# Gate and Up of the fourth token tile by Strassen's seven products, in a fused attention and gated feed-forward kernel

## The chip, the cores and the metric

The kernel runs on one core of a Trainium2 chip. Its time is the device time of one execution in microseconds, the median of several. TensorE (PE) multiplies matrices into banks of PSUM, VectorE (DVE) and ScalarE (ACT) read and empty those banks, GpSimd (POOL) works on SBUF alone, and SyncE (SP) issues the DMAs. Each engine takes its instructions in the order in which they stand in its queue; an instruction that has to wait holds up everything behind it on its engine.

## The reference

`x` has 2048 tokens of 512 elements. Both branches read the same normalised tokens. The inner width of the feed-forward, 1792, is 14 blocks of 128.

```python
xn = layernorm(x)                                  # 2048 x 512
q, k, v = split(xn @ wqkv)                         # 32 heads of 16
p = softmax(mask(q @ k.T * 16**-0.5))              # causal, window of 256
s = (p @ v) @ wo
gate, up = xn @ w1, xn @ w3                        # 2048 x 1792 each
h = silu(gate) * up
out = x + s * silu(h @ w2)
```

## The kernel before

Every float32 operand of a large product is split into two fp16 parts, high and low, and a product is made of three (high by high, low by high, high by low), so that one 128 by 128 block costs three matmuls.

The tokens are worked in four tiles of 512 (t = 0 to 3). The attention is cut into 32 units: a tile, a group of 8 heads and one half of it. A unit brings small score pieces (score products for the maxima, L671, and for the exponentials, L759) and one set of value products (L787), and around them stands dense work: projections (L601), values (L567), Gate and Up (L1059), Down (L1284, L1202) and the output projection (L1336). `spread` deals the dense pieces out between the score pieces of a unit, by a cost per piece; `feed_forward` lists the feed-forward's pieces, and each unit takes its share of the total. PE runs in exactly the order in which the program records its instructions. On the other engines a list scheduler sets the order, and pieces under `urgent()` go first.

`gate_up(t, f)` makes Gate, then Up, of one block f for all 512 tokens: 12 matmuls of 512 columns each, half of them per piece, into one PSUM bank. `bank()` hands out two banks in turn, m0 and m1, to all dense work. Gate is emptied by a tanh on ACT (L1074) and a product on DVE (L1078), Up by a product on DVE (L1083), which gives h.

Down is a plain product in tiles 0 and 1 (L1284). In tiles 2 and 3 it is already made by seven products: `fold_first` and `fold_second` form sums of h on POOL and split them into high and low parts (casts on ACT L1114 or POOL L1116, low parts on POOL L1117, sums L1125 and L1140 to L1142), `fold_weights` has made the sums of w2, and `fold_down_piece` runs the products (L1202, 256 columns each), which `unfold` adds up. Blocks 0 to 7 are one set of seven products, blocks 8 to 13 the second, in the order 0, 6, 3, 4, 5, 1, 2; the second set of tile 3 stands at the kernel's end, followed by the last output projections.

The scores of the exponentials go through a mask on DVE (L766) and an exponential on ACT (L769); the maxima are DVE instructions (L685). SBUF tiles named slot are one pool of 54, taken and given back.

## Time and profile before

| | |
|---|---|
| time, median of 3 runs | 803.87 us (803.73 to 803.97) |
| the profiled execution, first to last instruction (span) | 801.8 us |
| granted TensorE clock | 1.000 |
| PE busy | 791.1 us, 99% |
| DVE, ACT, POOL busy | 623.0, 393.9, 381.2 us (78, 49, 48%) |
| DMA | 134.18 MB, 167 GB/s in the mean |

The profile gives the profiled execution's own time as its span; the runs' median lies 2.07 us above that, which is what lies around the first and the last instruction. A row of a timeline gives the start, the length, the engine, the line and operation, what is written from what, and the count; in brackets stands how long the engine idled before it, and what ended that. Matmuls overlap: a 256-column matmul is listed with 0.27 us, but the next starts much earlier, so their cost is read from start to start.

### The profile page before, as it was taken

The page shows a single profiled execution, that of the slowest core. Times are in us where ns is not written, and L with a number is a line of the kernel's source. Part 1 is how long each engine was busy: PE and PEld are TensorE (multiplying, and loading weights), DVE is VectorE, ACT ScalarE, POOL GpSimd, SP SyncE. Part 2 cuts the span into 40 slices and gives each one's busy share as a digit, 9 for nine tenths or more (in the row PEclk, how much of TensorE's full clock was granted, in tenths as well). Part 3 has the DMA queues.
Part 4 walks back from the last instruction along what each step waited for, and adds up shares of the span by engine and source line. Part 5 has one row for each costly group of instructions (what it writes and reads, how often), then busy time and mean ns, then how long its engine had stood idle before and what let it go on. Part 6 is the DMA issues. An engine that isn't in the chain of part 4 may idle for free.

```text
span 801.8 us, 23974 instructions
## 1 busy us (share of the span) xinstructions
PE 791.1 (99%) x9181; PEld 403.8 (50%) x9181; DVE 623.0 (78%) x2005; ACT 393.9 (49%) x592; POOL 381.2 (48%) x746
## 2 busy tenths in 40 slices
PE   8999999999999999999999999999999999999997
PEld 4443445444454444444445444466544744466465
DVE  8887889778797778787888887776678876874537
ACT  6989777744355544344443344344434334444411
POOL 2355657633229435365442546330446276650770
PEclk9999999999999999999999999999999999999999
DMA  9987654636666565657555733665453553334431
GB/s 281 245 258 238 196 185 144 248 111 208 173 215 189 169 210 144 214 148 258 130 194 173 213 114 101 177 173 157 137 159 87 159 157 110 89 117 134 129 94 56
DMA packets 109858, 134.18 MB, mean 167 GB/s; under 512 B 18928, under 2 KB 64944, under 8 KB 109744
## 3 DMA queue, kind: packets, MB, share of 16 engines
q1 hardware_dynamic: 109456, 132.13, 55.4%
q8 instruction: 72, 1.18, 0.6%
q10 hardware_dynamic: 288, 0.52, 0.2%
q14 instruction: 42, 0.34, 0.1%
HBM read 91.23 MB, written 36.57 MB: 159 GB/s over the span
## 4 chain that ended last, share of the span: by engine, by line
PE 80%; DVE 8%; DMA 4%; ACT 3%; issue 2%; POOL 1%; SPq 1%; DVEq 0%; ACTq 0%; POOLq 0%
PE m L1059 31%; PE po L787 9%; PE m L601 8%; PE m L1202 8%; PE m L1284 7%; PE s L759 5%; PE m L1336 4%; PE m L567 4%; PE s L671 3%; DMA slot<-in_B_w_dram 2%; DVE junk L685 2%; PE po L671 2%; ACT sqa L249 1%; DVE s L766 1%; POOL slot L345 1%
## 5 line engine op out<-in xcount | busy, mean ns | idle before, releaser
L1059 PE MATMUL m<-XH,slot 128*128 128x512 f16 x896 | 267.3, 380 | 1.1 <-DVE slot L1078 0.6
L769 ACT ACTIVATE pt<-s,es 128x1024 f32<-128x1024 f32 x152 | 167.6, 1112 | 178.7 <-DVE s L766 176.9
L1059 PEld LDWEIGHTS <-slot 128*128 128x128 f16 x1344 | 124.9, 98 | 155.6 <-issue 13.1
L1059 PE MATMUL m<-XL,slot 128*128 128x512 f16 x448 | 169.8, 379 | 0.0
L766 DVE TENSOR_TENSOR s<-s,MK 128x256 f32<-128x256 f32 (+2 forms) x280 | 118.7, 434 | 53.5 <-PE s L759 49.8
L685 DVE CUSTOM_DVE_ANT_0 junk<-s,MW 128x320 bf16<-128x320 f32 x276 | 133.9, 485 | 18.4 <-PE s L671 11.4
L339 POOL TENSOR_TENSOR slot<-slot,slot 128x256 f16<-128x256 f32 (+1 forms) x86 | 57.6, 692 | 128.8 <-ACT slot L1092 60.0
L345 POOL TENSOR_TENSOR slot<-slot,slot 128x128 f16<-128x128 f32 x168 | 68.9, 444 | 76.6 <-ACT slot L343 76.6
L685 DVE CUSTOM_DVE_ANT_0 junk<-po,MW 128x320 bf16<-128x320 f32 x172 | 83.4, 485 | 4.6
L1284 PE MATMUL m<-slot,slot 128*128 128x512 f16 x336 | 78.5, 380 | 1.1 <-DVE slot L1078 1.1
L787 PE MATMUL po<-pt,V 64*32 64x320 f32 (+4 forms) x2880 | 77.2, 342 | 0.1
L601 PE MATMUL m<-XH,slot 128*128 128x512 f16 x240 | 70.8, 380 | 0.5 <-DVE slot L1078 0.5
L1202 PE MATMUL m<-slot,slot 128*128 128x256 f16 x588 | 68.4, 273 | 0.0
L1074 ACT ACTIVATE slot<-m,sgs 128x512 f32<-128x512 f32 x56 | 38.3, 684 | 59.8 <-PE m L1059 59.7
L1117 POOL TENSOR_TENSOR slot<-slot,slot 128x256 f16<-128x256 f32 x98 | 64.6, 671 | 1.1
L1202 PEld LDWEIGHTS <-slot 128*128 128x128 f16 x588 | 56.2, 98 | 11.5 <-issue 2.8
L787 PEld LDWEIGHTS po<-pt,V 64*32 64x32 f32 x2880 | 50.4, 106 | 22.4 <-issue 0.8
L1078 DVE SCALAR_TENSOR_TENSOR slot<-slot,m 128x512 f32<-128x512 f32 x56 | 38.3, 684 | 28.9 <-ACT slot L1074 26.7
L759 PE MATMUL s<-qa,KA 50*64 50x320 f16 (+3 forms) x1472 | 58.3, 259 | 0.0
L601 PEld LDWEIGHTS <-slot 128*128 128x128 f16 x392 | 36.5, 98 | 42.6 <-issue 1.7
L759 PEld LDWEIGHTS <-KA 50*64 50x64 f16 x1472 | 30.1, 105 | 51.7 <-issue 32.8
L1284 PEld LDWEIGHTS <-slot 128*128 128x128 f16 x336 | 30.7, 98 | 39.2 <-issue 4.7
(194 smaller groups left out, 1131.5 us busy)
## 6 DMA issues: line engine op xcount, KB each, us to landing
slot<-dW SPq DMA_DIRECT2D x98, 256.0 KB
slot<-in_B_w_dram SPq DMA_DIRECT2D x56, 256.0 KB
slot<-dFold SPq DMA_DIRECT2D x48, 256.0 KB
dW<-slot SPq DMA_DIRECT2D x42, 256.0 KB
slot<-in_A_x_dram SPq DMA_DIRECT2D x30, 256.0 KB
KA<-dK SPq DMA_DIRECT2D x24, 288.0 KB
slot<-dWQ SPq DMA_DIRECT2D x24, 256.0 KB
qa<-dQ SPq DMA_DIRECT2D x30, 192.0 KB
```

What stands on the lines that cost most here:

```text
L339: op(out[:, c], a[:, c], b[:, c])
L345: nc.gpsimd.tensor_sub(lo[:, c:c + P], raw[:, c:c + P], hi[:, c:c + P])
L601: nc.tensor.matmul(cell["pp"][:, cols[n]], w[:, (a * NC + c) * P:(a * NC + c + 1) * P], b[:, c, cols[n]], start=n == 0 and (c, i) == parts ...
L685: lasts["maximum"] = nc.vector.tensor_tensor_reduce(out=junk[:, :n], in0=s[:, r, :n], in1=mask, scale=1.0, scalar=NEG, op0=ALU.add, op1=AL ...
L759: nc.tensor.matmul(s[64 * h:64 * h + 64, r, o:o + 64 * n], ka[rows, 2 * p + a, 64 * (m + 4):64 * (m + 5)], qa[rows, 2 * p + a, 64 * (m + k ...
L766: nc.vector.tensor_add(v, v, MK[:, kind, of:of + n, :].unsqueeze(1).to_broadcast([P, 2 * len(which), n, 64]))
L769: lasts["exp"] = nc.scalar.activation(pt, s, AF.Exp, scale=es)
L787: nc.tensor.matmul(cell["po"][32 * i:32 * i + 32, h, 64 * (m + k):64 * (m + k + n)], V[64 * h:64 * h + 64, (4 * t + m // 2) % VB, hd * VW: ...
L1059: nc.tensor.matmul(cell[k], w[:, (a * NC + c) * P:(a * NC + c + 1) * P], b[:, c, :], start=c == 0 and i == 0, stop=c == NC - 1 and i == 2)
L1117: nc.gpsimd.tensor_sub(lo, view, hi)
L1202: nc.tensor.matmul(cell["ps"][:, c], made[:, f:f + P], wj[:, g:g + 256], start=j == j0 and c == 0 and n == 0, stop=j == j1 - 1 and n == 2, ...
L1284: nc.tensor.matmul(ps, hh[:, a * TW + b * P:a * TW + (b + 1) * P], w[:, c * D:(c + 1) * D], start=f == f0 and i == 0, stop=f == f1 - 1 and ...
```

## The change

Only the fourth tile's Gate and Up are changed. Two neighbouring blocks 2j and 2j+1 are taken together (a quad, j = 0 to 6). The weights of such a pair are a 2 by 2 arrangement (two halves of the 512 inputs by two blocks), the tokens another (two halves of the inputs by two halves of 256 tokens), and their product is made by seven products in place of eight, in Winograd's form with shared sums. One product is Gate in columns 0 to 255 and Up in columns 256 to 511 of one bank: 12 matmuls of 256 columns. Only products 1, 2 and 4 read plain weights; the sums of w1 and w3 are made on POOL in tiles 1 and 2 (`weight_sums`) and stored to DRAM, the sums of the tokens in tile 2 (`token_sums`).

The seven products stand in the order p1, p2, p6, p5, p7, p3, p4. p1, p6, p5 and p3 add up in one bank, m0, which the quad keeps (`retained`), and after each of them ACT copies the running sum out (L1421). p2, p7 and p4 go to the other bank; DVE adds one of those copies to them (L1426). Half a block of Gate and Up then lies in SBUF, and gets a tanh on ACT (L1436), a product on DVE (L1439) and one on POOL (L1440). `arranged` and `in_runs` place the quad's pieces among the other dense pieces: p1 with p2, p6 alone, p5 with p7, p3 with p4.

The scale of the normalised tokens is halved (XS) so that sums fit fp16, the weights' blocks are stored in another column order (`split_blocks`), the fold takes halves of the tokens in place of every second 128, and the third tile's output projections stand one unit later.

```diff
-XS = 2.0**10
+XS = 2.0**9
+QUAD_FROM = 3
+QUAD_AT = ((1, 10), (1, 13), (2, 1), (2, 3), (2, 5), (2, 7), (2, 9))
+HALVES_AT = {3: (2, 11)}
...
     def bank(shape, dtype=F32):
-        open_bank[0] = b = 1 - open_bank[0]
+        open_bank[0] = b = 1 - (open_bank[0] if retained[0] is None else retained[0])
...
+    def weight_sums(j):
...
+        def scale(i, k):
+            raw = cell["raw"][i][k]
+            with behind_exp():
+                nc.scalar.activation(raw, raw, AF.Copy, scale=inverses[:, j, k, i:i + 1])
+
+        def sums(k):
+            a, b = (cell["raw"][i][k] for i in range(2))
+            add(b[:, r], b[:, l], b[:, r])
+            sub(b[:, l], a[:, l], b[:, l])
+            sub(a[:, l], b[:, r], a[:, l])
+            sub(a[:, r], a[:, r], a[:, l])
+
+        def cut(i, k):
+            raw = cell["raw"][i][k]
+            made = take(F16)
+            with behind_exp():
+                nc.scalar.copy(made[:, 0:512], raw)
+            halves(sub, made[:, 512:], raw, made[:, 0:512])
...
+    LOADS = ((0,), (1,), (3, 4), (5, 6), (), (), (2,))
+
+    def quad(t, j):
...
+        def product(ps, w, x, first):
+            for k in range(2):
+                for c in range(2):
+                    for n, (a, b) in enumerate(((0, 0), (1, 0), (0, 1))):
+                        nc.tensor.matmul(ps[:, 256 * k:256 * k + 256], w(k, a, c), x(b, c),
+                                         start=first and k == 0 and c == 0 and n == 0,
+                                         stop=k == 1 and c == 1 and n == 2, skip_group_check=True)
+
+        def copied(ps):
+            made = take(F32)
+            with urgent():
+                lasts["exp"] = nc.scalar.activation(made, ps, AF.Copy, scale=CS)
+            return made
+
+        def added(ps, other):
+            with urgent():
+                lasts["emptied"] = nc.vector.scalar_tensor_tensor(other, ps, CS, other, op0=ALU.mult, op1=ALU.add)
+            return other
+
+        def activated(f, half, made, done_with=True):
...
+            nc.scalar.activation(h, made[:, 0:256], AF.Tanh, scale=sg_apart[:, f:f + 1])
+
+            def gated():
+                nc.vector.scalar_tensor_tensor(h, h, 1.0, made[:, 0:256], op0=ALU.add, op1=ALU.mult)
+                nc.gpsimd.tensor_mul(h, h, made[:, 256:512])
+                give(made, after=10)
+            later(1, gated)
...
+        def p6():
+            product(cell["a"], summed_up(0, 0), token_sum(1, 256), False)
+            cell["u2"] = copied(cell["a"])
+
+        def p5():
+            product(cell["a"], summed_up(1, 256), token_sum(0, 0), False)
+            cell["v5"] = copied(cell["a"])
+
+        def p7():
+            cell["b"] = bank([P, 512])
+            product(cell["b"], summed_up(1, 0), token_sum(0, 256), True)
+            give(QW[t, j, 5], QW[t, j, 6])
+            activated(o, 1, added(cell["b"], cell["v5"]))
+
+        def p3():
+            product(cell["a"], summed_up(0, 256), tokens(1, 256), False)
+            give(QW[t, j, 3], QW[t, j, 4])
+            retained[0] = None
+            activated(e, 1, copied(cell["a"]))
...
-        b = n % 8 - (2 if t < 3 else 3)
+        b = n % 8 - (2 if t < 3 else 4)
```

Three places show how the change moves instructions. The first is PE inside the third quad (j = 2 of tile 3), at the border of p6 and p5. Before, in Gate and Up of one block, a change of product is a change of bank, with 12 matmuls of 512 columns on each side (here the last of one bank and the first of the other):

```order
L1059 MATMUL m0_10730<-XH_3741,slot46_10341 128x512
L1059 LDWEIGHTS slot46_10341
L1059 MATMUL m0_10730<-XL_3742,slot46_10341 128x512
L1059 LDWEIGHTS slot3_10763 [waits DMAHW4_49]
L1059 MATMUL m1_10787<-XH_7565,slot3_10763 128x512 [waits DVE_49]
L1059 LDWEIGHTS slot3_10763
L1059 MATMUL m1_10787<-XH_7565,slot3_10763 128x512
```

Now:

```order
L1414 MATMUL m0_12251<-slot10_11185,slot14_12077 128x256
L1414 LDWEIGHTS slot14_12077
L1414 MATMUL m0_12251<-slot10_11185,slot14_12077 128x256
L1414 LDWEIGHTS slot52_12141 [waits DMAHW6_49]
L1414 MATMUL m0_12251<-slot27_11001,slot52_12141 128x256 [waits Activation_49]
L1414 LDWEIGHTS slot52_12141
L1414 MATMUL m0_12251<-slot27_11001,slot52_12141 128x256
```

p5 goes on in the bank that p6 has just filled, and waits for ACT, which has to copy it first.

The second place is ACT around the same point. Before, in the fourth tile, between two score pieces stand the tanh of a Gate (L1074), exponentials (L769) and casts of h (L1114), which wait for DVE:

```order
L1074 ACTIVATE slot45_11818<-m0_11805,sgs_155 128x512 [waits DMAHW4_49,PE_49]
L769 ACTIVATE pt_11837<-s_11826,es1_396 128x1024 [waits DVE_49,PE_49,Activation_49]
L1114 CAST slot13_11873<-slot45_11818 128x256 [waits DVE_49]
L1074 ACTIVATE slot25_11897<-m0_11884,sgs_155 128x512 [waits PE_49,Pool_49]
L769 ACTIVATE pt_11915<-s_11900,es1_396 128x1024 [waits DVE_49,PE_49,Activation_49]
L769 ACTIVATE pt_11932<-s_11917,es1_396 128x1024 [waits DVE_49,PE_49,Activation_49]
```

Now (L1421 copies a bank, L1436 is a tanh, L1135 a cast of h, L786 an exponential; the last row is the copy that p5 above waits for):

```order
L1436 ACTIVATE slot13_12066<-slot7_12226,sga_157 128x256 [waits Activation_49]
L1436 ACTIVATE slot33_12173<-slot50_12091,sga_157 128x256 [waits DVE_49]
L1421 ACTIVATE slot2_12264<-m0_12251 128x512 [waits PE_49]
L1135 CAST slot3_12295<-slot33_12173 128x256 [waits Pool_49]
L1436 ACTIVATE slot41_12289<-slot2_12264,sga_157 128x256 [waits DMAHW1_49,DVE_49]
L786 ACTIVATE pt_12317<-s_12302,es1_399 128x1024 [waits DVE_49,PE_49]
L786 ACTIVATE pt_12334<-s_12319,es1_399 128x1024 [waits DVE_49,PE_49]
L1421 ACTIVATE slot24_12361<-m0_12251 128x512 [waits PE_49]
```

The bank's copy stands behind two exponentials, and these behind a cast that waits for POOL.

The third place is POOL at the end, the sums of the last pair of blocks. Before (slot39 is h of block 12, slot3 of block 13; both come from DVE):

```order
L1125 TENSOR_TENSOR slot0_13359<-slot39_13339 128x256 [waits DVE_49]
L1116 CAST slot31_13358<-slot0_13359 128x256 [waits Pool_49]
L1117 TENSOR_TENSOR slot31_13358<-slot39_13339,slot31_13358 128x256 [waits Activation_49]
L1117 TENSOR_TENSOR slot31_13358<-slot0_13359,slot31_13358 128x256 [waits Pool_49]
L1140 TENSOR_TENSOR slot49_13457<-slot39_13339,slot3_13436 128x256 [waits DVE_49]
L1141 TENSOR_TENSOR slot49_13457<-slot49_13457,slot39_13339 128x256 [waits Pool_49]
L1117 TENSOR_TENSOR slot34_13461<-slot3_13436,slot34_13461 128x256 [waits PE_49,Activation_49]
```

Now (slot11 is h of block 12, slot21 of block 13; L1440 is the new product with Up, once per block and half):

```order
L1440 TENSOR_TENSOR slot21_14128<-slot21_14128,slot51_14110 128x256 [waits DVE_49]
L1138 TENSOR_TENSOR slot22_14223<-slot21_14128,slot22_14223 128x256 [waits DMAHW7_49,PE_49,Activation_49]
L1440 TENSOR_TENSOR slot11_14016<-slot11_14016,slot39_14148 128x256 [waits DVE_49]
L1146 TENSOR_TENSOR slot48_14193<-slot11_14016 128x256 [waits DMAHW2_49,Pool_49]
L1161 TENSOR_TENSOR slot23_14219<-slot11_14016,slot21_14128 128x256
L1137 CAST slot43_14192<-slot48_14193 128x256 [waits Pool_49]
L1162 TENSOR_TENSOR slot23_14219<-slot23_14219,slot11_14016 128x256 [waits Pool_49]
L1138 TENSOR_TENSOR slot43_14192<-slot48_14193,slot43_14192 128x256 [waits Pool_49]
L1137 CAST slot4_14254<-slot23_14219 128x256
L1440 TENSOR_TENSOR slot21_14128<-slot21_14128,slot50_14032 128x256 [waits DVE_49]
```

The sums of block 12 begin only after its second half, which comes from p3, the last product but one.

## Prediction

> **What bounds the kernel now.** I read the busy times first, then the same by stretches of the last two tiles (columns: PE, weight loads, DVE, ACT, POOL with counts, clock, DMA share, GB/s), then PE's waits.

> ```profile
> PE 791.1 (99%) x9181; PEld 403.8 (50%) x9181; DVE 623.0 (78%) x2005; ACT 393.9 (49%) x592; POOL 381.2 (48%) x746
> ...
> 400.00:500.00 100.00, 99.89 (x1255) 48.35 (x1254) 85.14 (x260) 41.33 (x55) 47.90 (x82) 1.00 0.55 162
> 500.00:600.00 100.00, 100.00 (x1294) 55.00 (x1292) 70.48 (x224) 41.78 (x54) 31.92 (x55) 1.00 0.59 161
> 600.00:650.00 50.00, 49.88 (x639) 29.35 (x639) 40.99 (x129) 17.86 (x21) 26.94 (x46) 1.00 0.42 124
> 650.00:700.00 50.00, 49.93 (x576) 23.33 (x575) 38.03 (x119) 20.79 (x31) 32.32 (x56) 1.00 0.42 118
> ...
> PE m L1284 <- DVE slot L1078: 1.1, 1, 1.1
> ```

> PE is full, at full clock, and its longest wait for anybody is 1.1 us in the whole run. So each microsecond of matmul taken out is worth a microsecond, and each new wait of PE costs one, since nothing else on PE has slack to take it up. DVE is at 80% or so beside it, in order, and this is what a hand-over from PE runs into.

> **What the products cost.** The timeline near the end has both shapes back to back: 24 matmuls of 512 columns, then 126 of 256.

> ```profile
> 768.07 0.60 PE L1059 MATMUL m<-XH,slot 128*128 128x512 f16 x2
> ...
> 773.26 13.92 PE L1202 MATMUL m<-slot,slot 128*128 128x256 f16 x126
> ...
> 787.01 5.34 PE L1336 MATMUL m<-slot,slot 128*128 128x512 f16 x24
> ```
> ```profile
> L1202 PEld LDWEIGHTS <-slot x588: 95/98/99, 523.3 to 786.8; 128*128 128x128 f16 x196
> L1202 PE MATMUL m<-slot,slot x588: 269/273/283, 523.5 to 786.9; 128*128 128x256 f16 x196
> ```

> From start to start that is 5.19 / 24 = 0.2163 us and 13.75 / 126 = 0.1091 us; the weight load of 0.098 us still fits under 0.109. Removed: 14 blocks by 24 matmuls, 336 by 0.2163 = 72.7 us. Added: 7 quads by 7 products by 12, 588 by 0.1091 = 64.2 us. PE saves **8.5 us**. This term is sure; what follows decides whether it is kept.

> **The shorter hand-over.** Before, a bank has 12 matmuls of 512 columns, 2.60 us, to be emptied while the other one fills. Now a product lasts 12 by 0.1091 = 1.31 us, and four of seven go into one bank, m0, which ACT must copy each time before the next may write. The durations, from the groups of the last 240 us:

> ```profile
> L769 ACT ACTIVATE pt<-s,es 128x1024 f32<-128x1024 f32 x48 | 52.6, 1113 | 46.8 <-DVE s L766 46.0 <-DVE NM L705 0.7
> L1074 ACT ACTIVATE slot<-m,sgs 128x512 f32<-128x512 f32 x19 | 13.0, 686 | 22.9 <-PE m L1059 22.9
> L1114 ACT CAST slot<-slot 128x256 f16<-128x256 f32 x29 | 10.8, 403 | 46.2 <-DVE slot L1083 46.2
> L1083 DVE SCALAR_TENSOR_TENSOR slot<-m,slot 128x512 f32<-128x512 f32 x19 | 13.1, 689 | 8.0 <-PE m L1059 8.0
> L1236 DVE TENSOR_TENSOR slot<-slot,slot 128x256 f32<-128x256 f32 x8 | 2.9, 414 | 0.0
> L1117 POOL TENSOR_TENSOR slot<-slot,slot 128x256 f16<-128x256 f32 x68 | 44.8, 671 | 0.8
> L1116 POOL CAST slot<-slot 128x256 f16<-128x256 f32 x39 | 15.4, 411 | 0.6
> L1125 POOL TENSOR_TENSOR slot<-slot 128x256 f32<-128x256 f32 x9 | 6.5, 727 | 5.8 <-DVE slot L1083 5.8
> ```
> ```profile
> 791.77 0.74 DVE L1340 SCALAR_TENSOR_TENSOR slot<-m,us,slot 128x512 f32<-128x512 f32 x1
> ...
> 792.56 2.75 PE L1336 MATMUL m<-slot,slot 128*128 128x512 f16 x12 [0.20 <-DVE slot L1340]
> ```

> A copy on ACT takes 0.69 us (L1074 has its shape), and PE follows 0.05 us after the end of what emptied its bank (791.77 + 0.74 to 792.56). A product's last matmul ends 0.273 - 0.109 = 0.16 us after the next could start. So the fastest hand-over is 0.16 + 0.05 + 0.69 + 0.05 = 0.95 us: it fits under one product, if ACT is free. But ACT stands behind exponentials, which wait for DVE's masks after each score piece. Three score pieces, with the dense work that resumes after each and the exponential's start:

> ```profile
> 638.67 4.11 PE L1202 MATMUL m<-slot,slot 128*128 128x256 f16 x36
> ...
> 640.52 1.12 ACT L769 ACTIVATE pt<-s,es 128x1024 f32<-128x1024 f32 x1 [7.12 <-DVE s L766]
> ...
> 647.34 0.41 PE L759 MATMUL s<-qa,KA 50*64 50x320 f16 x8
> ...
> 647.96 0.60 PE L601 MATMUL m<-XH,slot 128*128 128x512 f16 x2
> ...
> 649.09 1.11 ACT L769 ACTIVATE pt<-s,es 128x1024 f32<-128x1024 f32 x1 [2.19 <-DVE s L766]
> ...
> 652.66 0.60 PE L1059 MATMUL m<-XH,slot 128*128 128x512 f16 x2
> ...
> 653.67 2.19 ACT L769 ACTIVATE pt<-s,es 128x1024 f32<-128x1024 f32 x2 [0.18 <-DVE s L766]
> ```

> Counted from the resumption, ACT is through with its exponentials after 2.97 us (the piece that follows the values), 2.24 us (a plain one) and 3.20 us (one with two exponentials). With copy and return, 0.74 us more: 3.71, 2.98 and 3.94 us. Before, that was hidden under products of 2.6 us and their alternation. Now two products last 2.62 us, so PE waits 1.09, 0.36 and 1.32 us where two products stand between such a piece and the next use of m0, and 2.63 us where only one does. The new order on PE has these places:

> - plain piece, two products: p1 and p2 of quad 0, p3 and p4 of quads 1 and 4, p1 and p2 of quad 6: 4 by 0.36 = 1.4 us;
> - two exponentials, two products: p5 and p7 of quads 0 and 5, p3 and p4 of quad 3: 3 by 1.32 = 4.0 us;
> - after the values, two products: p1 and p2 of quad 1, p3 and p4 of quad 2: 2 by 1.09 = 2.2 us;
> - quad 2, p6 directly followed by p5 in the same bank: 2.6 us;
> - p6 to p5 with only a score piece of 0.62 us (647.34 to 647.96) between, quads 0, 1 and 4: 0.95 - 0.62 = 0.3 us each, 0.9 us.

> Together 11.1 us. Nothing below 0.9 us can come of it, since the last item needs no queue at all; above, DVE's own hand-overs (p7 to p4, p4 to the next p2: 14 of them, each at most one DVE instruction of 0.69 us late) would add up to 9.7 us. I take 0 for these, because p3 or p1 stands between, and DVE is freed by each wait that PE already has.

> **Casts that wait for POOL.** h now ends on POOL (L1440), so the cast of h on ACT waits for POOL's queue, and the exponentials behind it too. Per quad POOL gets 4 products more (2.9 us), which stand among the sums: the last product of a quad has one product and two sums ahead of it, so that a cast comes up to 4 by 0.727 = 2.9 us after DVE is done. Three such casts stand ahead of exponentials or copies for which PE soon waits (quads 2, 3 and 6). Between 0 (PE gets there later) and 2.9 us each I take 1 us: **3.0 us**.

> **The tail.** Before, no PE wait lies in the last 126 matmuls: block 12 is summed while block 13 is multiplied, and only block 13 is left.

> ```profile
> 772.19 0.34 DVE L834 RECIPROCAL dr<-dr 128x32 f32<-128x32 f32 x1
> ...
> 774.18 0.71 ACT L1114 CAST slot<-slot 128x256 f16<-128x256 f32 x2 [2.63 <-DVE slot L1083]
> 774.23 0.73 POOL L1140 TENSOR_TENSOR slot<-slot,slot 128x256 f32<-128x256 f32 x1 [4.48 <-DVE slot L1083]
> ...
> 780.06 0.67 POOL L1117 TENSOR_TENSOR slot<-slot,slot 128x256 f16<-128x256 f32 x1
> ```

> POOL needs 6.5 us for that (774.23 to 780.73), hidden under 13.8 us of products. Now both blocks' second halves come from p3 and p4, the last two products. Let p3 end at 0. DVE's product for block 13's second half ends at about 0.85 (behind a reciprocal as at 772.19), POOL's at 1.65, ACT's cast at 2.1; behind that cast stands the tanh of block 12's second half (2.5; a cast's 0.40 us taken for it), then DVE (2.95). POOL goes on with a low part (2.8), the product (3.7), two sums (5.2), a cast (5.6), a sum (6.3), and the low part that makes operand 6 (7.0). PE: p4 to 1.31, the first fold product of 18 matmuls to 3.27, a wait until DVE has emptied m1 behind its product (2.95 + 0.69 + 0.05: 0.4 us), 12 matmuls to 5.0, then 2.0 us of waiting. Operand 3 needs cast, product, low part, sum, cast, low part: 0.41 + 0.73 + 0.67 + 0.73 + 0.41 + 0.67 = 3.6, so 10.6; PE is there at 7.0 + 0.65 + 1.31 = 9.0: 1.6 us more. **4.0 us** in all. If POOL were at once free, two instructions less, 2.6; if the sums of the quad before were still in its queue, 6.

> **Edits that I take at nothing.** The sums of the weights: 7 by 16 POOL instructions, at 0.73 or 0.67 us about 78 us, and 7 by 8 of ACT; the rows from 400 to 600 us leave POOL some 120 us and ACT 117 us idle there. Without that cover a cast that waits for POOL holds the exponentials for a chain of four sums (2.9 us), as above: up to 4 us over tiles 1 and 2. DMA: 7 by (8 + 3) transfers of 256 KB more, about 20 MB, issued on SP ahead of use by a whole quad; the DMA share is 0.42 to 0.59. The other scale, column order, halves of tokens, the sums of the tokens (24 POOL instructions) and the output projections a unit later have the same counts or lie in idle time; if a load came late, PE would show it.

> **The sum.** 803.87 - 8.5 + 11.1 + 3.0 + 4.0 = **813.5 us** (in the profiled execution, 801.8 + 9.6 = 811.4 of span, the 2.07 us around it unchanged).

> **Rivals.** *The hand-overs hold* (faster). The place is m0 between two products; the point from which it decides is a copy that starts within 0.52 us of its product's end (1.31 - 0.95, and the 0.16 us that a last matmul overhangs). For it: ACT is only 36 to 42% busy in the rows above. Against: the order gives ACT two exponentials ahead of the copy, and the rows show when those end. Then only 0.9 us and the tail remain: 803.87 - 8.5 + 0.9 + 4.0 = 800.3 us.

> *Half of it.* If the masks come earlier because DVE is no longer held by the second emptying of a bank, half of the 11.1 us goes, and POOL holds nobody: 803.87 - 8.5 + 5.5 + 4.0 = 804.9 us, no change that can be told.

> *POOL becomes the bound.* Per quad it has 4 products, 3 more sums and 1 (L1125), 7 low parts and 4 casts: 8 by 0.727 + 7 by 0.671 + 4 by 0.411 = 12.2 us, and quads 1 to 4 stand close, with about 59 us of PE work (4 by 9.2 of products, the rest scores, values and two output projections, by their rows) and 49 us of POOL's, to which the normalisation and the output projections' adds come. Late casts then cost their 2.9 us each (5.7 us more), and POOL meets DVE:

> ```profile
> 656.24 0.73 POOL L1116 CAST slot<-slot 128x256 f16<-128x256 f32 x2
> ...
> 701.82 1.24 POOL L1116 CAST slot<-slot 128x256 f16<-128x256 f32 x2
> ...
> 702.10 0.69 DVE L1331 SCALAR_TENSOR_TENSOR slot<-slot,slot 128x512 f32<-128x512 f32 x1 [1.44 <-ACT slot L1330]
> ```

> Two casts that take 0.73 us took 1.24 while DVE worked on two SBUF operands: 0.5 us lost. The change adds 28 such DVE products (L1439) right beside POOL's; at 0.1 us of PE each, 2.8 us. 813.5 + 5.7 + 2.8 = 822 us.

> [...]

> That the change doesn't do what it says is excluded for PE's count (588 for 336 stand in the order).

> **How the numbers follow.** My forecast 0.60, with its own range 807 to 819 (tail 2.6 to 6, POOL's casts 0 to 6, hand-overs 8 to 14). The hand-overs hold: 0.14. Half: 0.09. POOL: 0.17. This measurement tells 0.2%, 1.6 us, from no change: faster 0.15, same 0.08, slower 0.77. The range 802 to 821 leaves out most of the first rival and half of the last.

> **What would show it.** In the profile after: the new product line with idle time ended by ACT's copy line, 8 us or more in all; ACT's copies starting behind exponentials; one gap of some 2.6 us between p6 and p5 of quad 2; PE idle twice, for 2.0 and 1.6 us, in the last fold products, ended by POOL; PE's busy time lower by about 8.5 us. If PE's idle time in the fourth tile stays under 8 us in sum, I am wrong; the copies' start after their product's end says in which step.

## The result: 6.5% slower

The changed kernel takes 856.47 us (four runs, 853.33 to 859.71) against 803.92 before: 1.065 times as long, with a 95% interval of 1.0618 to 1.0682. Slower was forecast, but with 813.5 us and a range up to 821; 52.6 us were lost instead of 9.6. Of one kernel below, the quads with the product on DVE, one execution of four took 997.5 us at a clock of 0.75 and is left out; it is the profiled one, so the table has dashes there.

The busy times and two of the rows of slices from the page of the profile after (span 851.5 us):

```profile
PE 794.8 (93%) x9433; PEld 432.5 (51%) x9433; DVE 636.6 (75%) x2027; ACT 443.9 (52%) x694; POOL 495.9 (58%) x910
PE   8999999999999999998979999599999888889887
PEclk9999999999999999999989999799999999999999
```

PE is no longer full, and its busy time has not fallen by 8.5 us but risen by 3.7. The slices show two regions with holes: single ones in three slices, the 19th, the 21st and the 26th (the last is 532 to 553 us), all before the first product of a quad at 646 us; and a thin spread from 660 us on, in the fourth tile. The same by stretches, with the columns of the prediction's first fence:

```profile
400.00:500.00 100.00, 92.77 (x1175) 44.82 (x1175) 82.13 (x237) 47.44 (x67) 64.91 (x112) 0.97 0.61 185
500.00:600.00 100.00, 88.34 (x1121) 49.32 (x1120) 63.40 (x198) 46.61 (x65) 72.62 (x116) 0.95 0.64 196
...
700.00:800.00 100.00, 88.21 (x1229) 64.36 (x1227) 61.35 (x174) 47.19 (x74) 60.52 (x96) 0.98 0.45 138
```

From 400 to 600 us, where PE was 99.89 and 100.00 us busy before, it now idles 18.9 us and is granted less than the full clock. What ended PE's waits, in order of size (total, times, longest):

```profile
PE m L618 <- DMA slot<-dWQ: 9.8, 1, 9.8
PE m L1414 <- ACT slot L1421: 9.1, 8, 2.8
PE m L1080 <- DMA slot<-dW: 5.2, 1, 5.2
PE s L688 <- ACT pt L786: 4.3, 7, 1.5
PE m L1223 <- DMA slot<-dFold: 2.2, 1, 2.2
PE s L688 <- DVE M L702: 2.1, 2, 1.9
```

Three of these six are ended by DMA, where before none was: loads of weights for a projection (dWQ), for Gate and Up (dW) and for the fold (dFold), all of which the kernel had before. The account of the profiled execution, from windows of 5 us: the span grew by 49.7 us, of which 20.9 are idle time of PE between 300 and 600 us, 23.8 idle time after 600, 1.2 before 300, and 3.7 busy time. In the last, 8.5 us of matmuls are gone and 6.3 us were added by the lower clock (the sum of busy time times one less the granted clock); the remaining 5.9 us I put down to matmul ends, by the prediction's estimate that the last matmul before a break overhangs by 0.16 us (0.273 less 0.109); that last part is argued, not measured apart.

**The largest hole.** PE at 537 us, then SP's issues in the same stretch (a start, a length, the line, what is loaded or stored; in rows of SP the idle time is not printed, it is the gap between two rows):

```profile
537.18 0.31 PE L688 MATMUL s<-KA,qa 48*64 48x320 f16 x4
547.25 1.03 PE L618 MATMUL m<-XH,slot 128*128 128x512 f16 x2 [9.76 <-DMA slot<-dWQ]
```
```profile
528.09 0.40 SPq L853 DMA_DIRECT2D de<-dr  x1
532.69 1.58 SPq L1328 DMA_DIRECT2D dSum<-slot  x2
534.44 0.32 SPq L895 DMA_DIRECT2D slot<-dW  x1
534.85 4.36 SPq L859 DMA_DIRECT2D rb<-de  x8
539.26 2.88 SPq L1200 DMA_DIRECT2D slot<-dFold  x6
542.18 0.43 SPq L653 DMA_DIRECT2D slot<-dWQ  x1
```

The load that PE waits for is issued 4.7 us after PE has stopped for it. Ahead of it on SP stand two stores of the new sums (L1328), which held SP from 528.5 to 532.7 us until POOL had finished them, and 15 older transfers. After its issue another 5.1 us pass before PE starts: six loads for the fold stand just ahead of it, and the DMA share, 0.32 from 538 to 540 us, is 0.93 to 1.06 in each us from 541 to 547. So about half of this hole lies before the issue, and the other half where the loads that were held up run together on the DMA engines. Worked out for the 11 loads of dWQ after 400 us, the time from issue to the first matmul was 30.4 us in the median before and is 9.0 us now.

### The profile page after: what moved, and what is told of

It is laid out like the page before. It is cut to its first block, busy times and chain, and to the rows that moved or that the text cites. A ratio compares the mean times of both kernels' runs of the same rounds, so it can differ in the third digit from the quotient of the medians.

```text
span 851.5 us, 24929 instructions
## 1 busy us (share of the span) xinstructions
PE 794.8 (93%) x9433; PEld 432.5 (51%) x9433; DVE 636.6 (75%) x2027; ACT 443.9 (52%) x694; POOL 495.9 (58%) x910
## 4 chain that ended last, share of the span: by engine, by line
PE 56%; DVE 12%; POOL 11%; ACT 8%; issue 6%; DMA 5%; SPq 3%; ACTq 0%; POOLq 0%; DVEq 0%
PE m L1080 18%; PE m L618 7%; PE po L804 6%; PE m L1528 6%; PE m L1223 5%; PE s L776 4%; PE m L584 3%; DVE junk L702 3%; ACT pt L786 2%; PE m L1580 2%; POOL slot L347 2%; PE s L688 2%; POOL slot L1138 2%; DVE s L783 2%; POOL slot L1440 1%
## 5 line engine op out<-in xcount | busy, mean ns | idle before, releaser
L786 ACT ACTIVATE pt<-s,es 128x1024 f32<-128x1024 f32 x152 | 167.4, 1112 | 180.8 <-DVE s L783 172.9
L1080 PE MATMUL m<-XH,slot 128*128 128x512 f16 x672 | 201.5, 382 | 5.7 <-DMA slot<-dW 5.2
L347 POOL TENSOR_TENSOR slot<-slot,slot 128x256 f16<-128x256 f32 (+1 forms) x150 | 99.8, 690 | 108.1 <-ACT slot L1113 49.5
L1080 PEld LDWEIGHTS <-slot 128*128 128x128 f16 x1008 | 93.6, 98 | 122.6 <-issue 11.4
L1080 PE MATMUL m<-XL,slot 128*128 128x512 f16 x336 | 127.8, 381 | 0.0
L618 PE MATMUL m<-XH,slot 128*128 128x512 f16 x240 | 72.1, 386 | 11.7 <-DMA slot<-dWQ 9.8
L363 POOL TENSOR_TENSOR slot<-slot,slot 128x128 f16<-128x128 f32 x112 | 46.6, 450 | 47.1 <-DMA dQ<-slot 26.4
L1138 POOL TENSOR_TENSOR slot<-slot,slot 128x256 f16<-128x256 f32 x98 | 66.1, 683 | 10.8 <-ACT slot L1135 9.5
L1414 PEld LDWEIGHTS <-slot 128*128 128x128 f16 x588 | 56.5, 98 | 23.1 <-issue 15.3
L1223 PEld LDWEIGHTS <-slot 128*128 128x128 f16 x588 | 56.9, 99 | 18.0 <-issue 5.3
L618 PEld LDWEIGHTS <-slot 128*128 128x128 f16 x392 | 36.3, 99 | 54.9 <-DMA slot<-dWQ 12.1
L776 PEld LDWEIGHTS <-KA 50*64 50x64 f16 x1472 | 30.6, 106 | 52.7 <-issue 31.6
L688 PE MATMUL s<-KA,qa 48*64 48x320 f16 (+3 forms) x824 | 45.7, 296 | 6.7 <-ACT pt L786 4.3
L1528 PEld LDWEIGHTS <-slot 128*128 128x128 f16 x336 | 30.7, 98 | 40.3 <-issue 6.4
```

What stands on the lines that cost most here:

```text
L347: op(out[:, c], a[:, c], b[:, c])
L618: nc.tensor.matmul(cell["pp"][:, cols[n]], w[:, (a * NC + c) * P:(a * NC + c + 1) * P], b[:, c, cols[n]], start=n == 0 and (c, i) == parts ...
L688: nc.tensor.matmul(s[c:c + w, r, :n], qa[rows, 2 * p + a, ii * P + c:ii * P + c + w], ka[rows, 2 * p + a, e - n:e], start=True, stop=True)
L776: nc.tensor.matmul(s[64 * h:64 * h + 64, r, o:o + 64 * n], ka[rows, 2 * p + a, 64 * (m + 4):64 * (m + 5)], qa[rows, 2 * p + a, 64 * (m + k ...
L786: lasts["exp"] = nc.scalar.activation(pt, s, AF.Exp, scale=es)
L1080: nc.tensor.matmul(cell[k], w[:, at:at + P], b[:, c, :], start=c == 0 and i == 0, stop=c == NC - 1 and i == 2)
```

## The experiments

All times are beside runs of the kernel before on the same chip (803.8 to 804.1 us). "Idle" is PE's, "clock" is what the lower granted clock added, both from windows of 5 us of the profiled execution; the kernels are described below. Of the kernel with dashes only the time is used. In the rows quoted, line numbers are shifted by a few where a kernel has lines more or fewer.

| kernel | us | over before | ratio, 95% | idle 300–600 | idle after 600 | PE busy | clock |
|---|---|---|---|---|---|---|---|
| before | 803.92 | | | 0.2 | 4.6 | 791.1 | 0.0 |
| after | 856.47 | 52.6 | 1.0618–1.0682 | 21.1 | 28.4 | 794.8 | 6.3 |
| quads alone | 828.17 | 24.1 | 1.0283–1.0314 | 1.2 | 27.2 | 791.9 | 2.5 |
| preparation alone | 817.99 | 13.9 | 1.0153–1.0189 | 9.4 | 7.8 | 794.6 | 1.7 |
| its transfers alone | 815.83 | 11.7 | 1.0119–1.0167 | 6.8 | 5.9 | 794.5 | 2.7 |
| its POOL and ACT work alone | 814.86 | 10.8 | 1.0117–1.0151 | 7.4 | 5.5 | 794.5 | 1.8 |
| quads and transfers | 840.04 | 36.0 | 1.0420–1.0463 | 12.3 | 25.5 | 795.1 | 8.2 |
| quads and the sums' work | 835.40 | 31.4 | 1.0366–1.0416 | 7.2 | 26.9 | 791.0 | 2.7 |
| quads, no POOL product | 815.69 | 11.6 | 1.0122–1.0165 | 1.2 | 17.5 | 785.9 | 0.0 |
| quads, product on DVE | 819.66 | 15.7 | 1.0184–1.0218 | – | – | – | – |
| quads, two banks | 826.70 | 22.6 | 1.0259–1.0290 | 1.2 | 26.4 | 788.6 | 1.7 |
| before, 46 slots | 834.75 | 30.8 | 1.0344–1.0423 | 11.7 | 9.2 | 802.6 | 9.4 |
| after, late stores | 852.54 | 48.4 | 1.0582–1.0614 | 17.6 | 29.2 | 797.4 | 7.4 |
| after, earlier loads | 848.85 | 44.7 | 1.0517–1.0592 | 12.7 | 29.2 | 798.1 | 10.0 |
| after, fewer slots | 851.71 | 47.7 | 1.0578–1.0609 | 19.6 | 29.6 | 794.4 | 5.8 |
| fewer slots, earlier loads | 854.78 | 50.8 | 1.0609–1.0647 | 19.6 | 30.5 | 795.4 | 7.2 |

### Which half of the change costs

The preparation alone: the fourth tile is made block by block as before, the sums of the weights are still made and stored.

```diff
-QUAD_FROM = 3
+QUAD_FROM = 4
...
```

> The sums of the weights and of the tokens are made and stored as in the changed kernel, but the fourth tile is multiplied as before, block by block (the sums are never read). In the trace of the change the last gate and up block of the third tile begins 31.6 us later than before. Theory (tiles 1 and 2 lose their time to the making of the sums): 803.9 + 30 = 834 us, between 828 and 838, with the two long waits of PE on loads of dW and dWQ. Rival, as the prediction had it (the sums lie in idle time, at most 4 us): 804 to 808 us; then what is lost before the fourth tile comes from the loads for the quads.

The quads alone: no sums of weights are made; the quads load parts of plain weights in their place.

```diff
-            lasts["load"] = nc.sync.dma_start(made, dSum[(i - 3) // 2, (i - 3) % 2, j])
+            lasts["load"] = nc.sync.dma_start(made, dW1[2 * j + (i - 3) // 2, (i - 3) % 2])
...
-            if (t, at) in sums_at:
+            if False:
```

> The quads stay, with the sums of the tokens, but no sums of weights are made: in their place the quads load parts of the split weights of the same size, so that the products are others and the output is not the reference's. Theory: what remains is the fourth tile's own cost, 803.9 - 8.5 + 25 (PE's idle time after 640 us in the trace of the change, some 2 us of it as before) + 4 (a product's last matmul overhangs by 0.16 us at each of some 25 more breaks) + 2 (a lower clock after gaps) = 825 us, between 820 and 829. Rival, as the prediction had it: 813.5 less the 3 us of casts that wait for a full POOL, 810 us.

Measured: 13.9 us for the preparation alone, 24.1 us for the quads alone. The quads' figure was met; for the preparation neither theory's was. The two add up to 38.0 of 52.6 us: beside the quads the preparation costs 28.3 us (856.47 less 828.17), twice what it costs beside the old fourth tile. The table shows that the two halves cost at different places: the quads alone leave PE full up to 600 us, and most of the preparation's idle time lies before that (9.4 us from 300 to 600 us, against 0.2 before). Both kernels keep the change's smaller edits (scale, column order, sums of the tokens, later output projections), which no run has alone; as the quads alone idle only 1.2 us from 300 to 600 us, these cost little there.

**Transfers or work?** With the old fourth tile, and then beside the quads, either only the transfers of the preparation (loads, and stores of what was loaded) or only its work on POOL and ACT, on ones in place of weights:

```diff
 its transfers alone (POOL's sums, ACT's scalings and casts left out)
+                    with behind_load():
+                        nc.sync.dma_start(dSum[i, k, j].bitcast(F32), raw)
 its work alone (loads and stores left out)
-                    lasts["load"] = nc.sync.dma_start(raw[i][k].rearrange("p (c f) -> p c f", f=P),
...
-                    nc.sync.dma_start(dSum[i, k, j], made)
```

> As the run with the sums made and the fourth tile as before, but only the transfers of the weights' sums are left: w1 and w3 are loaded and stored again as they came, same sizes, same number, and neither POOL nor ACT touches them. Theory A (SP's queue is held because a store waits for POOL): 804 to 810 us, no long wait of PE on a load. Rival B (the transfers themselves, their share of the DMA engines or of SP's issue time, make the other loads late): most of the 30 us, 825 to 835 us.

> As the run with the sums made and the fourth tile as before, but without the transfers of the weights' sums: POOL and ACT do the same instructions on ones, and nothing is loaded or stored for them. Theory A (stores that wait for POOL hold SP): 804 to 812 us. Rival C (POOL's and ACT's work itself holds the casts and the exponentials, and through them DVE and PE): 820 to 835 us, with PE waiting on ACT and DVE, not on loads.

> The run with the quads alone (828.2 us) and beside it only the transfers of the weights' sums: w1 and w3 loaded and stored again as they came, never read. With the fourth tile as before the transfers alone took 11.7 us. Theory T (they shorten the lead of the ordinary loads from some 28 to some 8 us, and that is nearly the whole cost): 843 to 853 us. Rival (it takes POOL's late work too): 830 to 840 us.

> The run with the quads alone (828.2 us) and beside it only the sums' work on POOL and ACT, on ones, without a transfer. With the fourth tile as before it took 10.8 us. Theory T: the loads keep their lead, so no more than that: 830 to 840 us. Rival (POOL's and ACT's work is the cause): 843 to 853 us.

Beside the old fourth tile the transfers cost 11.7 us and the work 10.8, together 13.9. Beside the quads they cost 11.9 and 7.2, together 28.3, so that 9.2 us arise only where both are there. Beside the old fourth tile neither run fell into a range that had been foretold; beside the quads the work did, and the transfers came to the upper edge of the lower one. Both runs also hold slots for the sums, so slots are not separated from transfers or work here. PE's waits with the transfers alone beside the quads, then with the work alone beside the old fourth tile:

```profile
PE m L618 <- DMA slot<-dWQ: 7.2, 3, 5.4
PE m L1080 <- DMA slot<-dW: 4.7, 1, 4.7
```
```profile
PE s L776 <- DMA KA<-dK: 6.4, 1, 6.4
```

The first is the wait for late loads again, 11.9 us without any sum on POOL. The second says more: no transfer was added here at all, and yet PE waits for a load, from 507.2 to 513.6 us. SP ahead of it:

```profile
495.90 0.36 SPq L653 DMA_DIRECT2D slot<-dWQ  x1
500.19 4.22 SPq L1200 DMA_DIRECT2D slot<-dFold  x3
504.52 2.78 SPq L739 DMA_DIRECT2D qa<-mt  x4
507.40 0.38 SPq L645 DMA_DIRECT2D dK<-slot  x1
507.83 0.47 SPq L646 DMA_DIRECT2D dK<-slot  x1
...
509.99 0.82 SPq L664 DMA_DIRECT2D KA<-dK  x2
```

From 496.3 to 504.4 us SP issues three fold loads only, since each goes into a slot that POOL has yet to read (3.8 and, in two, 3.7 us of SP's waits in this stretch); what PE waits for stands behind them. So the work on POOL, with the slots that it holds, turns into late loads, as more transfers do.

### What makes the loads late

**Stores that wait for POOL** were the first theory for the kernel after. The stores are planned 22 steps later, so that POOL is through when SP comes to them:

```diff
-            later(8, store)
+            later(30, store)
```

> The changed kernel, but each store of a weight sum (L1328) comes 30 steps after its low part is planned, and not 8, so that POOL has long made it when SP reaches the store. Theory A (stores that wait for POOL hold SP's queue, and the loads behind them are late): SP's 14.6 us of waits at L1328 go, and with them most of PE's 9.8 us at 547 us and some of the lower clock behind it: 856.5 - 13 = 843 us, 838 to 847. Rival (the loads are late by the number of transfers in the queue, or because POOL's work holds the slots of other loads): 852 to 858 us.

852.54 us: 4 us better, and PE's wait for dWQ is still 8.9 us. The store that holds SP at 528.5 is one delay of several; in sum SP waited less for POOL between 300 and 600 us in the kernel after (20.1 us) than before (36.7).

**The loads are asked for too late.** The projections' weights two units ahead in place of one, Gate's and Up's three blocks ahead in place of two:

```diff
-                        pieces += [(0, lambda t=t, f=f: load(t, f)) for f in range(2)]
-                    if f + 2 < FB:
-                        pieces.append((0, lambda t=t, f=f + 2: load(t, f)))
+                        pieces += [(0, lambda t=t, f=f: load(t, f)) for f in range(3)]
+                    if f + 3 < FB:
+                        pieces.append((0, lambda t=t, f=f + 3: load(t, f)))
...
-                if u == n + 1 and tiles[k][0]:
+                if u == n + 2 and tiles[k][0]:
```

> The changed kernel, but each load of dWQ is issued two units ahead of its use and not one (some 20 us earlier), and each pair of loads of dW three blocks ahead and not two. Theory L (the loads ran some 10 us ahead of PE, and whatever holds SP for longer ends in a wait of PE): PE's waits for dWQ and dW, 9.8 and 5.2 us, go, and some 3.5 us of lower clock behind them: 856.5 - 18 = 838 us, 833 to 843. Rival (the loads can't come earlier, because their slots come free late or the DMA engines are full): 850 to 858 us.

848.85 us, 7.6 better. The wait for dWQ is gone (34.2 us from issue to use in the median), the one for dW is not (4.7 us), and a load that comes earlier also holds its slot longer.

**The slots.** The kernel before with 8 of its 54 slots taken away, and nothing else changed; and the kernel after with w1's half of a pair worked off before w3's is loaded, so that half as many slots are held:

```diff
 before
-SLOTS = 54
+SLOTS = 46
 after
-    def weight_sums(j):
+    def weight_sums(j, k):
...
-            cell["raw"] = raw = [[take(F32) for _ in range(2)] for _ in range(2)]
+            cell["raw"] = raw = [take(F32) for _ in range(2)]
```

> The kernel before with 46 of the shared 256 KB buffers (slots) in place of 54, nothing else. The weight sums hold some eight slots at a time for long; in the program of the change 60 slots between the middle of tile 1 and the middle of tile 2 are taken again before their planned rest is over, where the kernel before has none there, and a load into such a slot stands later in SP's order. Theory S (what the sums take from the other loads is slots): fewer slots alone, without a transfer or an instruction more, make loads late: 809 to 819 us. Rival (POOL's work and SP's transfers do it): 802 to 806 us.

> The changed kernel with the same sums, instructions and transfers, but w1's and w3's half of a pair are loaded, summed and stored one after the other, with shorter rests, so that the sums hold about half as many slots (18 early takes in that stretch in place of 60, 13 of them there without any weight sums). Theory S: the preparation's share, 28.3 us (856.5 less the 828.2 of the quads alone), falls to some 10 us: 838 us, 833 to 843. Rival (transfers and POOL's work): 850 to 858 us.

PE's waits of the kernel before with 46 slots:

```profile
PE m L601 <- DMA slot<-dWQ: 16.1, 4, 5.8
PE m L1202 <- DMA slot<-dFold: 4.0, 2, 3.5
```

Eight slots fewer cost 30.8 us, where at most 15 had been foretold, with the same two kinds of late load as in the kernel after, although no transfer and no instruction was added. That slots alone can cost as much as the whole preparation is shown. That they are what the preparation costs is not: with half the slots the kernel after gains 4.8 us; the wait for dW at 430 us is gone, and the wait for dWQ at 535 us is 11.1 us.

**Both.** Fewer slots and earlier loads, the first dW loads of the third tile among them:

```diff
-                    if f == 0:
+                    if f == 0 and t == 1:
                         pieces += [(0, lambda t=t, f=f: load(t, f)) for f in range(2)]
+                    if f == FB - 2 and t == 1:
+                        pieces += [(0, lambda f=f: load(2, f)) for f in range(2)]
...
-                if u == n + 1 and tiles[k][0]:
+                if u == n + 2 and tiles[k][0]:
```

> The changed kernel with half as many slots held by the sums (as in the run with fewer slots), each load of dWQ two units ahead of its use, and the first two blocks' loads of dW of the third tile issued two blocks before the second tile ends. Theory L (the ordinary loads have lost their lead, and what holds SP for some us then ends in a wait of PE): the waits of 5.2 and 9.8 us and the lower clock behind them go, 836 us, 831 to 841. Rival (the sums' work on POOL and ACT delays casts and exponentials whatever the lead): PE's waits move to ACT and DVE, 844 to 852 us.

854.78 us, 3.1 more than with fewer slots alone: the theory of the lead falls as the whole cause. PE waits for none of these loads any more, and as long for something else. ACT and PE at that place:

```profile
564.39 0.69 ACT L1237 ACTIVATE slot<-m,fd 128x512 f32<-128x512 f32 x1 [5.90 <-DMA dSum<-slot]
```
```profile
565.13 2.72 PE L1223 MATMUL m<-slot,slot 128*128 128x256 f16 x12 [9.87 <-ACT slot L1237]
```

The copy that empties a bank of the fold got a slot out of which a sum was still being stored, and PE waits for the bank. So what the earlier loads took away comes back through the slots.

**Another queue.** All 56 transfers of the preparation issued from POOL, or from ACT, in place of SP:

```diff
-                    lasts["load"] = nc.sync.dma_start(raw[i][k].rearrange("p (c f) -> p c f", f=P),
+                    lasts["load"] = nc.gpsimd.dma_start(raw[i][k].rearrange("p (c f) -> p c f", f=P),
...
-                    nc.sync.dma_start(dSum[i, k, j], made)
+                    nc.gpsimd.dma_start(dSum[i, k, j], made)
```

> The changed kernel, with the loads of w1 and w3 for the sums and the stores of the sums issued from POOL and not from SP; all else the same. In the new order SP's loads of dW stand ahead of the denominators' transfers again, as with the quads alone. Theory P (the transfers take the ordinary loads' places in SP's queue): the 11.9 us of the transfers and the 9 us by which both together exceed their sum go: 856.5 - 20 = 836 us, 831 to 842. Rival (slots and POOL's work, which stay): 848 to 857 us.

> The same with all 56 transfers issued from ACT. Theory P: 836 us as above, if nothing on ACT waits behind them. Rival: each store on ACT waits there for POOL's low part, and the tanh, copies and exponentials behind it too, so that it is no better than with SP: 850 to 865 us.

889.37 us (1.1042 to 1.1079) and 874.64 us (1.0836 to 1.0901): 33 and 18 us worse than from SP, and worse than any range foretold. From POOL's case the group of the 28 loads (busy time, mean ns, idle time before them), and a row of DVE:

```profile
L1303 POOL DMA_DIRECT2D slot<-in_B_w_dram x28 | 22.0, 787 | 51.4 <-issue 31.2 <-DMA dSum<-slot 6.7 <-PE m L1223 4.8
```
```profile
560.61 0.35 DVE L851 RECIPROCAL dr<-dr 128x32 f32<-128x32 f32 x1 [12.43 <-DMA dr<-os]
```

Ahead of these loads POOL did nothing for 51.4 us in all, and the issue of one takes it 0.79 us. One such gap, of 4.46 us, ends at 540 us; from then to 566 us POOL has only one gap more, of 0.32 us. A cast on ACT waits 12.11 us there for one of POOL's sums, and SP waits 10.7 us for POOL between 543 and 558 us, ahead of the transfer that DVE waits for. So a transfer at the head of POOL's queue holds POOL's own work behind it, and what waits for that on ACT and on SP. From ACT it is the other way round: 21 of its stores waited there for POOL, 43 us in all.

### The fourth tile

The quads alone, as above, are the base here. PE's waits in it:

```profile
PE m L1414 <- ACT slot L1421: 10.0, 10, 2.9
PE s L688 <- ACT pt L786: 3.4, 6, 1.5
PE s L688 <- DVE M L702: 2.3, 2, 1.9
```

**POOL's product.** It is left out, or made on DVE instead:

```diff
 left out
-                nc.gpsimd.tensor_mul(h, h, made[:, 256:512])
 on DVE
-                nc.gpsimd.tensor_mul(h, h, made[:, 256:512])
+                nc.vector.tensor_mul(h, h, made[:, 256:512])
```

> The run with the quads alone (828.2 us), without POOL's product with Up at L1440 (left out, so that h is another). The prediction's term (casts that wait for POOL's product): 3.0 us less, 825 us. The prediction's rival (POOL is the bound of the fourth tile, by late casts and by the two engines' sharing of SBUF): 8.5 us less, 820 us. Rival (POOL's product holds nobody that PE waits for): 827 to 829 us.

> The run with the quads alone (828.2 us), with the product with Up at L1440 on DVE and not on POOL. Theory Q (what costs is that ACT's casts stand before the tanh and the exponentials and wait for POOL's queue, 28.3 us in sum there): near the run without the product (815.7 us), with the product's time on DVE where it is hidden: 816 to 820 us. Rival (DVE at 77% has no room: 28 by 0.41 us = 11.5 us more ahead of its masks): 824 to 830 us.

Without it the kernel takes 815.69 us, 12.5 less; on DVE 819.66, 8.5 less, although DVE then has 28 instructions more. So the place of the product costs, more than the product. Of the 12.5 us, 2.5 are the lower clock, which is gone without the product. ACT's waits from 600 us on, with the product on POOL and without it:

```profile
ACT pt L786 <- DVE s L783: 38.2, 20, 7.5
ACT slot L1135 <- POOL slot L1440: 28.3, 12, 4.4
```
```profile
ACT pt L786 <- DVE s L783: 46.6, 25, 7.5
ACT slot L1436 <- DVE slot L1426: 16.4, 18, 1.6
```

Twelve casts of h waited for POOL, 28.3 us in all, up to 4.4 us each. How one of them reaches PE, in the timeline of the quads alone (POOL's product, ACT's cast and the tanh behind it, DVE's product and a maximum behind it, then the score piece):

```profile
714.83 0.73 POOL L1440 TENSOR_TENSOR slot<-slot,slot 128x256 f32<-128x256 f32 x1
...
715.60 0.40 ACT L1135 CAST slot<-slot 128x256 f16<-128x256 f32 x1 [2.95 <-POOL slot L1440]
...
715.91 0.50 ACT L1436 ACTIVATE slot<-slot,sga 128x256 f32<-128x256 f32 x1
...
716.45 0.42 DVE L1439 SCALAR_TENSOR_TENSOR slot<-slot,slot 128x256 f32<-128x256 f32 x1 [1.81 <-ACT slot L1436]
...
717.31 0.49 DVE L702 CUSTOM_DVE_ANT_0 junk<-s,MW 128x320 bf16<-128x320 f32 x1
...
717.87 0.33 PE L688 MATMUL s<-KA,qa 48*64 48x320 f16 x4 [1.89 <-DVE M L702]
```

The cast holds a tanh of another half block, that holds DVE's product, and behind that stand the maxima which have to empty the score bank before PE may write the next piece. The same exchange in the whole kernel (after with fewer slots, then that with earlier loads too) gave 844.32 and 846.37 us, 7.4 and 8.4 less than without it:

> The changed kernel with both edits: half as many slots for the sums, and the product with Up on DVE. If the two causes add up: 856.5 - 18 - 10 = 828 us, 822 to 834, still slower than before. If they are one and the same (POOL's load), no more than the larger of the two alone.

> The run with lead and slots, and the product with Up on DVE. If the two causes are separate, 7 to 8 us less than that run, 828 us if it comes to 836: still slower than the 804 us of before, since the short hand-overs, the tail and the overhang of each product remain.

The gain by DVE, 7.4 to 8.5 us, is there each time, whatever the loads do. Both are still 5% slower than before, and the first missed the 822 to 834 us that had been foretold, because fewer slots had gained only 4.8 us.

**The retained bank.** In the quads alone, the four products that add up in m0 go to alternating banks and do not add up (as many matmuls and copies are made):

```diff
 p6, and p5, p3 and p4 alike
-            product(cell["a"], summed_up(0, 0), token_sum(1, 256), False)
+            cell["a"] = bank([P, 512])
+            product(cell["a"], summed_up(0, 0), token_sum(1, 256), True)
```

> The run with the quads alone (828.2 us), but each product goes to the other bank than the one before and starts it afresh (no product is added onto the one in its bank, so the values are others; the copies and additions are the same in number and size). The prediction's step (a product that follows in the same bank waits out the whole copy): the gap between p6 and p5 of the third quad, 2.87 us in the trace, and those of the other quads, 1.07, 1.03 and 0.2 us, go: 828.2 - 5 = 823 us. Rival (the copy is as late as before, so the wait only moves to the next use of its bank, 1.3 us of product later): 826 to 829 us.

826.70 us, 1.5 less; the intervals of the two (1.0259 to 1.0290 and 1.0283 to 1.0314) overlap, so this may be nothing. In the third quad p6 and p5 now run through, and p7, which takes the bank that p6 had, waits instead:

```profile
681.94 1.47 PE L1414 MATMUL m<-slot,slot 128*128 128x256 f16 x12 [1.55 <-ACT slot L1421]
```

That is the 2.86 us of before less the 1.31 us of one product: the copy comes as late, and the wait has only moved to the next use of its bank. The waits for the copies fall from 10.0 to 7.8 us in all. The bank matters little: the copy comes late because of what stands ahead of it on ACT.

## Why the prediction was wrong in size

**Right.** The price of the matmuls came out as reckoned. Within a product the 588 new matmuls of the kernel after start 0.1093 us apart in the mean, which makes 64.3 us where 64.2 were reckoned. Without the POOL product, where the clock is 1.00 throughout, PE's busy time is 785.9 us, 5.2 below before; the overhang at some 20 more breaks (0.16 us each, argued) would be the rest of the 8.5 us. The hand-overs of m0 were priced at 11.1 us and measured 9.1 (10.0 in the quads alone), and 8.7 of them at the places that were named; p6 to p5 of the third quad was 2.6 by the prediction and 2.84. The tail was 4.0 and is 3.2.

That these two sums come so close is in part luck, since their parts are off in both directions. The wait behind p5 and p7 of quad 5 is 2.25 us where 1.32 were priced, and the three borders of p6 and p5 that were to cost 0.3 us each, "needs no queue at all", show no wait. In the tail DVE's wait is 1.5 us where 0.4 was priced, and POOL's two are 0.8 and 0.9 where 2.0 and 1.6 were.

**"Casts that wait for POOL: 3.0 us."** The mechanism was right, the term was mis-sized: it measured 12.5 us by leaving the product out (with the clock's 2.5) and 7.4 to 8.5 by moving it. The prediction counted three casts and 1 us each; there were twelve, up to 4.4 us, and behind a cast stood not only exponentials but the tanh of the next half block, by which the wait passes over to DVE and to the maxima. The rival in which POOL becomes the bound had this at 8.5 us more than the forecast, which is close to what leaving the product out gave over the forecast (9.5); as a forecast for the whole kernel, 822 us, it fails too.

The rival's second half, that POOL and DVE hold each other up, hides in the means. DVE's product among the groups of the quads alone, and then without POOL's product:

```profile
L1439 DVE SCALAR_TENSOR_TENSOR slot<-slot,slot 128x256 f32<-128x256 f32 x28 | 16.4, 588 | 16.1 <-ACT slot L1436 16.1
```
```profile
L1439 DVE SCALAR_TENSOR_TENSOR slot<-slot,slot 128x256 f32<-128x256 f32 x28 | 16.3, 583 | 9.5 <-ACT slot L1436 9.4
```

588 against 583 ns looks like nothing. But where no POOL instruction, or only the last 0.1 us of one, runs at its start, this instruction takes 0.36 to 0.43 us; where one runs, it ends 0.28 us after POOL's. One such pair of the quads alone, POOL's sum to 695.91 and DVE's product to 696.18:

```profile
695.18 0.73 POOL L1146 TENSOR_TENSOR slot<-slot 128x256 f32<-128x256 f32 x1
...
695.47 0.71 DVE L1439 SCALAR_TENSOR_TENSOR slot<-slot,slot 128x256 f32<-128x256 f32 x1 [0.57 <-ACT slot L1436]
```

So it is in 17 of the 18 such cases of the quads alone (0.277 to 0.284 us) and in all 16 of the kernel after (0.279 to 0.285 us); the 18th, at 665.19, took 2.69 us. Counted above 0.42 us, this took 4.7 us of DVE's time in the quads alone and 4.5 without POOL's product, where only POOL's other instructions run beside it. So it is not what the product costs; what grew with the product is the idle time ahead of DVE, 9.5 to 16.1 us.

**"Edits that I take at nothing: the sums of the weights."** This is the step that failed, with 28.3 us where up to 4 were allowed. The bound was made from sums of idle time, some 120 us of POOL and of ACT from 400 to 600 us, and from the DMA share. Both were right as sums: ACT and POOL are still only 47% and 65 to 73% busy there. What counted was not read: how long before its use each older load was issued (30.4 us in the median), what in SP's order stood ahead of it, and how many of the 54 slots were free. The new transfers and the new sums took that lead, by SP's order and by the slots, for loads that the change does not touch. "Issued on SP ahead of use by a whole quad" was true of the new loads, and the wrong loads were looked at.

**The clock.** It has no term in the prediction's sum: 6.3 us in the kernel after, 2.5 in the quads alone, none before. See below.

**What stays open.** How the 28.3 us divide between SP's order, the slots and the time of the transfers on the DMA engines. Late stores, earlier loads and fewer slots each gained 4 to 8 us, the last two together gained 1.7, and moving the transfers to another queue lost 18 to 33. Each of the edits that kept SP's queue took away or shortened one of the late loads, and another wait came up or grew. The order of all engines but PE is made by the scheduler, and changes with each edit, so that an experiment here never changes one wait alone. An order of SP by due time of each load was not tried.

## What to carry to other kernels

Where the bounding engine has no slack, "hidden under idle time" has to be shown per wait, not per engine: for each in-order queue that new work joins (the DMA issues above all) read the shortest lead of the loads behind it, and count the buffers that are free at the worst moment. An intermediate step that is put on a shared engine costs by what stands in order behind whoever waits for it (here 28 products on POOL, 0.75 us each, had ACT wait 28.3 us), and moving it to a busier engine can be the cheaper choice (8.5 us less here). A gap of TensorE can cost more than its length: in the quads alone one of 2.86 us was followed by half the clock, and the 24 matmuls behind it took 4.45 us in place of 2.78.

## What the hardware showed unexpectedly

```profile
682.03 4.45 PE L1414 MATMUL m<-slot,slot 128*128 128x256 f16 x24 [2.86 <-ACT slot L1421]
```
```profile
673.55 5.07 PE L1223 MATMUL m<-slot,slot 128*128 128x256 f16 x30 [2.21 <-DMA slot<-dFold]
...
709.20 2.78 PE L1414 MATMUL m<-slot,slot 128*128 128x256 f16 x24 [2.84 <-ACT slot L1421]
```

The same 24 matmuls at the same place take 4.45 us in one and 2.78 in the other, after gaps of the same length: the first paid 1.67 us on top of its 2.86. The windows of 1 us of the second gap (PE, weight loads, DVE, ACT, POOL, clock, DMA share, GB/s):

```profile
674.00:675.00 1.00, 1.00 (x6) 0.71 (x5) 0.00 (x0) 0.00 (x0) 0.00 (x0) 0.50 0.98 259
...
676.00:677.00 1.00, 1.00 (x7) 0.70 (x6) 0.00 (x0) 0.00 (x0) 0.00 (x0) 0.55 0.86 315
677.00:678.00 1.00, 1.00 (x11) 0.90 (x10) 0.65 (x1) 0.00 (x0) 0.00 (x0) 1.00 0.65 162
```

Half the clock is granted there from 673.49 to 676.90 us. In the whole trace of the kernel after it falls five times, at 431.14, 540.37, 673.49, 762.24 and 850.98 us; the fifth time the kernel ends before it comes back. The nine changes lie whole multiples of 3.413 us apart, within 1 ns.

The length of a gap does not tell which of them this follows: it followed gaps of 2.21 and 2.86 us, and not one of 2.84. In the 3.413 us that end at a fall, PE had idled 2.94, 2.89, 2.16, 1.80 and 2.98 us. Divided in the same steps, the trace has 236 stretches at full clock behind which the clock stayed full; in these PE idled 2.00 us or less. The gap of 2.21 us has 2.15 us in the stretch from 670.08 to 673.49, that of the quads alone 2.68 in the 3.41 us up to the fall at 682.76; that of 2.84 is divided at 707.62 into 1.26 and 1.58 us. Ahead of the fall at 762.24 stand two short gaps, 1.46 us and the first part of another one, 1.80 together. As one stretch with 2.00 us (from 799.78) kept the clock and this one with 1.80 lost it, the idle time of a stretch does not settle it between those two. In the last 3.413 us before the clock came back, PE had idled 0.34 us or less.
